# Attention, low-rank mix and MLP on one core: all 24 two-head steps ahead of the first layer, in a new order

## The chip, the cores and the metric

One core of a Trainium2 chip runs the whole program in one launch. The metric is device microseconds (us) of that core from the start to the end of an execution; 0.2% of it, about 1.8 us, is roughly what a measurement of this kernel can tell from no change.

## What is computed

The reference, cut to what matters (B = 4 batches, H = 12 heads, S = 448 positions, D = 64, model width 768, hidden width 3072, rank 32):

```python
scores = q @ k.T / sqrt(64)                    # per batch and head, causal mask
attn   = exp(scores - rowmax)
attn   = attn / (attn.sum(-1) + 1e-9)
x      = attn @ v                              # heads side by side: (B, S, 768)
h      = x.transpose(0, 2, 1) @ U @ V          # mix along the sequence, rank 32
u      = x + h.transpose(0, 2, 1)
out    = u + relu(u @ w_ch1) @ w_ch2           # 768 -> 3072 -> 768
```

## The kernel before

**Stages.** The program has three. First comes attention with the low-rank mix. Then the first layer (`mlp`) computes the MLP of batches 0 and 1, in 8 parts of 6 weight blocks: 192 small steps of 9 TensorE matmuls each, 1728 in all, each 128x128 by 128x448. Last comes the second layer (`strassen`), which does batches 2 and 3 with Strassen products. The weights arrive as 64-bit words that VectorE, ScalarE and GpSimd decode to 32-bit floats, block after block; a decoded block is written back to memory (`kept`) for the second layer.

**Attention.** The work is tiled in 24 pairs of heads (b, c), 6 per batch. A pair needs these operations, each a small function:

- `load_qk`, `load_v`: transfers, issued by SyncE (SP) in the order of the program.
- `scores` (L219): 8 score blocks of TensorE into six PSUM banks, tile `s`.
- `scores_max` (L234): VectorE scales, masks, takes the row maximum and writes `p` to SBUF, 8 times a pair (4 row tiles of 112 for each of 2 heads).
- `scores_exp` (L248): ScalarE, 8 times. `sums_inverse` (L255 adds 1e-9, L256 reciprocal): VectorE, twice. `normalise` (L261): GpSimd, 8 times.
- `transposes` (L272): 20 TensorE transposes in six groups (two heads, three parts), tile `t`; `transposed` copies each group from PSUM to `pt` in SBUF, three parts a head, the table `ENG` naming the engine (L164 ScalarE, L166 VectorE).
- `values` (L288): TensorE, tile `pv`; `values_out` (L164): ScalarE copies it to `x` (tiles `xa`, `xb`).
- `x_natural` (L320): four TensorE transposes of `x`, tile `xt`; `natural_high` (L324, ScalarE) and `natural_low` (L329, VectorE) split them into a high and a low part, `xn_h` and `xn_l`.
- For every second pair `low_rank` (L337, TensorE, tile `y`) and its split (L346 ScalarE, L350 VectorE).
- For each batch, when its six pairs are through, six times `mix` (L355, L356, TensorE, tile `hm`) and `mix_sum` (L360, VectorE); for batches 0 and 1 also `split_u` and `split_u_low` (L168, L172, GpSimd), the operands of the first layer.

**What sets the order.** Nothing is scheduled by the compiler: each engine runs its instructions in the order in which Python emits them. `attention()` makes the list `todo` from a table `plan`. In step n every operation works on pair n minus its lag: scores, maxima and exponentials lag 0, transposes lag 1, values and `x` transposes lag 2, low rank lag 3, mix later. In the old table one operation of `plan` is emitted for all its tiles at once. The list is cut at `START = 18`: steps 0 to 17 run ahead of the first layer, and the rest is emitted in pieces between the matmul groups of the first layer, spread over its first 132 small steps (`UFREE = 60` of 192 stay free). After it `u_rounds` prepares operands of the second layer, one round every `UGAP = 3` small steps. PSUM tiles come from a pool of 8 banks, shared by attention and first layer. The decoding of U and V (`low_rank_weights`) and of weight blocks 0 and 1 (`decode_w`) is put behind whole steps (`VU_AT`, `W_AT`).

Of the kernel before, what the change touches and what calls it, by code (L numbers as in the profile page):

```python
# [12 lines left out]
I32 = mybir.dt.int32  # L13
U32 = mybir.dt.uint32
AF = mybir.ActivationFunctionType
# [4 lines left out]
P = 128  # L20
# [20 lines left out]


ENG = {
    "h0": "A", "h1": "A", "h2": "V", "vc": "A",
    "uh": "P", "ul": "P",
}

MIX, MIXN = 4, 2
START = 18
VU_AT = (0, 2, 3, 4)
UFREE = 60
UGAP = 3
LOADS = (13, 11, 7)
PREPS = (7, 5, 3)

WE = "PVVP"
HE = {"d": "V", "o": "V", "13": "V", "24": "V"}  # L60
UE = {"d": "P", "o": "P", "13": "P", "24": "V"}
WL_AT = (1, 2)
W_AT = (7, 8, 9, 10, 11)


@with_exitstack
def attention_mix_mlp(ctx: ExitStack, tc: tile.TileContext, qk, v, w1, w2, vu, out):
# [26 lines left out]
    def apool(name, bufs, **kw):  # L94
        return att.enter_context(tc.tile_pool(name=name, bufs=bufs, side="right", **kw))

    const = apool("const", 1)
    p_qk = apool("p_qk", 3)
    p_v = apool("p_v", 2)
    p_pt = apool("p_pt", 2)  # L100
    p_p = apool("p_p", 4)
    p_sm = apool("p_sm", 6)
# [13 lines left out]
    def f(ap):  # L116
        return ap.bitcast(F32)
# [23 lines left out]
        nc.sync.dma_start(out=t[:, :n].rearrange("p a b -> p (a b)"), in_=src.bitcast(U32))  # L141
        return t

    def decode_bits(t, n):

        lo, hi = t[:, :n, 0], t[:, :n, 1]
        st["nwa"] = st.get("nwa", -1) + 1
        a = main.tile([P, WB], U32, tag=f"wa{st['nwa'] % 2}", name="wa")[:, :n]
        nc.scalar.activation(f(a), f(hi), AF.Abs)
        nc.vector.tensor_scalar(f(a), f(a), HI_MIN, HI_MAX, op0=ALU.max, op1=ALU.min)  # L150
        nc.vector.tensor_scalar(a, a, 3, 0x3FFFFFF8, op0=ALU.logical_shift_left, op1=ALU.bitwise_and)
        nc.vector.scalar_tensor_tensor(hi, hi, 0xC0000000, a, op0=ALU.bitwise_and, op1=ALU.bitwise_or)  # L152
        nc.scalar.activation(lo.bitcast(I32), lo, AF.Copy, scale=2.0**-29)
        return a

    def decode_sum(t, a, n):
# [17 lines left out]
    def split(src, hi, lo):  # L174
        nc.scalar.copy(hi, src)  # L175
        nc.vector.tensor_tensor(lo, src, f(hi), op=ALU.subtract)  # L176

    def low_rank_weights(step):
        if step == 0:
            st["vu"] = load_words(vu, VCOLS)  # L180
        elif step == 1:
            st["vua"] = decode_bits(st["vu"], VCOLS)
        elif step == 2:
            decode_sum(st.pop("vu"), st["vua"], VCOLS)
        else:
            a = f(st.pop("vua"))
            split(a[:, :S], vm_h, vm_l)
            u = a[:CP, S:].rearrange("p (s r) -> p s r", s=NT)
            for i in (0, 2):
                split(u, um_s[:, :, i, :], um_s[:, :, i + 1, :])  # L190

    def load_qk(b, c):

# [79 lines left out]
    def transposed(b, h, part):  # L275
        n = (4, 3, 3)[part] * CP
        t = st["pt", b, h, part] = p_pt.tile([CP, n], F32, tag=f"pt{part}", name="pt")
        copy(f"h{part}", t, st.pop(("t", b, h, part))[:, :n])

    def values(b, c):  # L280
        v = st.pop(("v", b, c))
# [102 lines left out]
    def load_w(n):  # L384
        if n < len(blocks):
            st["wr", n] = load_words(blocks[n], WB)

    def decode_w(n, step):
        if n >= len(blocks):
            return  # L390
        if step == 0:
            st["wa", n] = decode_bits(st["wr", n], WB)
        elif step == 1:
            decode_sum(st.pop(("wr", n)), st["wa", n], WB)
            nc.sync.dma_start(out=kept[n], in_=f(st["wa", n]))
        else:
            o = NC * 2 * S + n % 2 * 2 * WB
            wh, wl = wsp[:, o : o + WB], wsp[:, o + WB : o + 2 * WB]
            split(f(st.pop(("wa", n))), wh, wl)
            st["w", n] = wh, wl  # L400

    def decode_ahead(blk, quarter):
        if quarter == 0:
# [463 lines left out]

    def attention():


        def of_pair(f, lag):
            def steps(n):
                if 0 <= n - lag < len(pairs):
                    yield f, pairs[n - lag]

            return steps

        def of_tiles(f, half, lag, tiles):
            def steps(n):
                if 0 <= n - lag < len(pairs):  # L880
                    b, c = pairs[n - lag]
                    for i in tiles:
                        yield f, (b, 2 * c + half, i)

            return steps

        def of_head(f, half, lag):
            def steps(n):
                if 0 <= n - lag < len(pairs):
                    b, c = pairs[n - lag]  # L890
                    yield f, (b, 2 * c + half)

            return steps

        def of_two(f, lag):
            def steps(n):
                if 0 <= n - lag < len(pairs) and (n - lag) % 2:
                    b, c = pairs[n - lag]
                    yield f, (b, c // 2)

            return steps

        def mixes(f, part):
            def steps(n):
                for b in range(B):
                    for c in range(NC):
                        if n == b * NPAIR + NPAIR - 1 + MIX + c // MIXN and c % MIXN == part:
                            yield f, (b, c)

            return steps  # L910

        def only(f, *a):
            b, _ = a
            if b < 2:
                f(*a)

        def third(half):
            plan = []
            for i in range(3):
                plan.append(of_tiles(transposes, half, 1, (i,)))  # L920
                plan.append(of_tiles(transposed, half, 1, (i,)))
            return plan

        first, second = (0, 2, 3, 1), (1, 3, 2, 0)
        plan = [
            of_pair(load_qk, -2),
            of_pair(scores, 0),
            of_tiles(scores_max, 0, 0, first),
            of_tiles(scores_exp, 0, 0, first),
            of_pair(natural_low, 3),  # L930
            of_tiles(scores_max, 1, 0, second),
            of_tiles(scores_exp, 1, 0, second[:2]),
            of_pair(values, 2),
            of_pair(values_out, 2),
            of_head(sums_inverse, 0, 0),
            of_tiles(normalise, 0, 0, first),
            *third(0),
            of_tiles(scores_exp, 1, 0, second[2:]),
            of_pair(x_natural, 2),
            of_head(sums_inverse, 1, 0),  # L940
            of_tiles(normalise, 1, 0, second),
            *third(1),
            of_two(low_rank, 3),
            of_two(low_rank_high, 3),
            of_two(low_rank_low, 3),
            of_pair(natural_high, 2),
        ]
        for part in range(MIXN):
            plan += [mixes(mix, part), mixes(mix_sum, part)]
        plan.append(of_pair(load_v, 1))  # L950
        for part in range(MIXN):
            plan += [mixes(lambda *a: only(split_u, *a), part), mixes(lambda *a: only(split_u_low, *a), part)]

        def scores_and_max(b, c):
            scores(b, c)
            for half, i in SCORES:
                scores_max(b, 2 * c + half, i)

        def nothing(*_):
            pass  # L960

        among = {scores: scores_and_max, scores_max: nothing}
        todo = []
        for n in range(-2, len(pairs) + 8):
            for steps in plan:
                todo += [(n, f if n < START else among.get(f, f), a) for f, a in steps(n)]
        return todo

    with tc.manual_schedule():
        constants()  # L970
        early = [(n, low_rank_weights, (i,)) for i, n in enumerate(VU_AT)]
        early += [(n, load_w, (i,)) for i, n in enumerate(WL_AT)]
        for n, steps in zip(
            W_AT,
            (
                [(decode_w, (0, 0))],
                [(decode_w, (0, 1)), (load_w, (2,))],
                [(decode_w, (0, 2))],
                [(decode_w, (1, 0))],
                [(decode_w, (1, 1)), (load_w, (3,))],  # L980
            ),
        ):
            early += [(n, step, a) for step, a in steps]
        early.sort(key=lambda e: e[0])
        todo = attention()
        while todo[0][0] < START:
            n, step, a = todo.pop(0)
            step(*a)
            while early and early[0][0] <= n:
                _, step, a = early.pop(0)  # L990
                step(*a)


        steps = 4 * FS * (FC + NC // 2)
        free = steps - UFREE
        done = 0
        us = None
        for i, _ in enumerate(mlp()):
            while done < len(todo) and done * free < len(todo) * (i + 1):
                _, step, a = todo[done]  # L1000
                step(*a)
                done += 1
# [62 lines left out]
```

## Time and profile before

| what | value |
|---|---|
| time, median of 3 runs (lowest to highest) | 907.77 us (907.39 to 908.99) |
| the profiled execution: its own time | 908.52 us |
| the profiled execution: span of the profile | 906.7 us |
| granted TensorE clock, mean over the span | 0.982 of full speed |
| busy share: TensorE / VectorE / ScalarE / GpSimd | 96% / 75% / 52% / 35% |
| first matmul of the first layer | at 165.26 us |
| second layer begins | at 584.5 us |

Times inside the profile are us from the start of the span. The profile's span and the execution's own time differ by 1.8 us, which lies around the span. "Busy" of an engine is the time in which at least one of its instructions runs; TensorE's matmuls overlap one another, so the distance between the starts of two groups tells more than their durations. Engine names in rows: PE is TensorE (PEld its weight loads), DVE VectorE, ACT ScalarE, POOL GpSimd, SP SyncE.

### The profile page before, as it was taken

To read this page: it belongs to the slowest core of one execution; us is meant where nothing else is said; L and a number is where in the kernel's file an instruction comes from. 1 tells how busy PE (TensorE), PEld (TensorE's weight loads), DVE (VectorE), ACT (ScalarE), POOL (GpSimd) and SP (SyncE) were. 2 spreads that over 40 slices of the span, in tenths; PEclk is the share of its full clock that TensorE was granted. 3 is DMA by queue.
4 is the path that set the end of the run, shared out by engine and by line. 5 is a ranking of instruction groups with operands and counts; after the bars stand their busy time and mean duration, and the time that the engine had idled before them with its cause. 6 is when DMAs were issued, how large, how long until landed. Compare 5 with 4: busy or idle time off the path is not lost.

```text
span 906.7 us, 13562 instructions
## 1 busy us (share of the span) xinstructions
PE 868.4 (96%) x4728; PEld 759.0 (84%) x4728; DVE 681.3 (75%) x1368; ACT 474.9 (52%) x1002; POOL 318.8 (35%) x342
## 2 busy tenths in 40 slices
PE   6798889999999999999799999999999999999998
PEld 4676667888888888888699999998999898898887
DVE  5566767756666676756458788879988989988896
ACT  6888778644544545354234545365453635445530
POOL 4444756542223313131014334323423423423220
PEclk9899899999999999999999999999999999999999
DMA  7224143235444334344234445721211221212103
GB/s 247 63 82 124 43 133 93 74 123 169 153 139 161 132 119 153 130 143 146 83 105 157 157 167 199 240 58 56 85 53 35 86 67 42 74 47 71 35 1 122
DMA packets 47061, 98.99 MB, mean 109 GB/s; under 512 B 4240, under 2 KB 25744, under 8 KB 46992
## 3 DMA queue, kind: packets, MB, share of 16 engines
q1 hardware_dynamic: 46992, 98.12, 33.1%
q8 instruction: 37, 0.61, 0.3%
q14 instruction: 32, 0.26, 0.1%
HBM read 73.73 MB, written 24.38 MB: 108 GB/s over the span
## 4 chain that ended last, share of the span: by engine, by line
PE 39%; DVE 9%; ACT 2%; issue 1%; DMA 1%; SPq 0%; DVEq 0%; ACTq 0%
PE sa L656 13%; PE of L449 7%; PE hf L424 7%; PE se L656 7%; PE sb L656 3%; DVE h L470 2%; DVE tmp L470 1%; DVE sw L470 1%; DVE xb L470 1%; DVE wsp L470 1%; ACT h L478 1%; DVE r L470 1%; DMA v<-in_v_dram 1%; ACT wsp L593 0%; PE pv L288 0%
## 5 line engine op out<-in xcount | busy, mean ns | idle before, releaser
L449 PE MATMUL of<-g,wsp 128*128 128x448 f32 x864 | 184.5, 368 | 0.0
L470 POOL TENSOR_TENSOR wsp<-wld,wsp 128x512 fp32r<-128x512 f32 (+1 forms) x60 | 105.3, 1764 | 214.6 <-ACT wsp L593 131.4
L449 PEld LDWEIGHTS of<-g,wsp 128*128 128x128 f32 x864 | 159.9, 188 | 13.0 <-DVE g L433 0.2
L157 POOL TENSOR_TENSOR wa<-wld 128x768 int32<-128x768 int32 (+1 forms) x49 | 73.1, 1492 | 247.4 <-DVE wld L152 123.0
L261 POOL TENSOR_SCALAR p<-p,r 112x112 f32<-112x112 f32 (+1 forms) x192 | 99.7, 538 | 106.6 <-DVE r L256 55.2
L248 ACT ACTIVATE p<-p,m 112x112 f32<-112x112 f32 (+1 forms) x192 | 100.3, 525 | 28.8 <-DVE m L234 28.2
L656 PE MATMUL sa<-h,wsp 128*128 128x448 f32 x432 | 98.6, 367 | 1.9 <-DVE xb L470 1.9
L424 PE MATMUL hf<-u,wsp 128*128 128x448 f32 x432 | 96.4, 373 | 0.0
L424 PE MATMUL hf<-wsp 128*128 128x448 f32 x432 | 94.4, 368 | 0.0
L656 PE MATMUL sa<-uch,wsp 128*128 128x448 f32 x288 | 89.5, 371 | 3.4 <-ACT r L677 3.4
L656 PEld LDWEIGHTS sa<-h,wsp 128*128 128x128 f32 x432 | 80.6, 188 | 10.6 <-DVE xb L470 3.8
L424 PEld LDWEIGHTS hf<-u,wsp 128*128 128x128 f32 x432 | 80.9, 191 | 6.9
L452 DVE TENSOR_TENSOR xa<-of,xa 128x448 f32<-128x448 f32 x96 | 58.7, 620 | 36.8 <-PE of L449 36.4
L424 PEld LDWEIGHTS hf<-wsp 128*128 128x128 f32 x432 | 80.2, 188 | 7.0 <-issue 0.3
L234 DVE CUSTOM_DVE_ANT_0 p<-s,mask 112x112 f32<-112x112 f32 (+2 forms) x192 | 74.2, 444 | 14.1 <-PE s L219 12.3
L175 ACT CAST wsp<-wa 128x768 fp32r<-128x768 f32 x48 | 40.2, 837 | 83.8 <-POOL wa L157 75.6
L433 DVE SCALAR_TENSOR_TENSOR g<-hf,g 128x448 fp32r<-128x448 f32 x48 | 29.9, 623 | 62.5 <-ACT g L432 62.4
L432 ACT ACTIVATE g<-hf 128x448 fp32r<-128x448 f32 x48 | 26.2, 546 | 78.0 <-PE hf L424 77.9
L272 PE MATMUL t<-ident,p 112*112 112x112 f32 x480 | 63.2, 272 | 3.7 <-POOL p L261 2.1
L176 DVE TENSOR_TENSOR wsp<-wa,wsp 128x768 fp32r<-128x768 f32 x48 | 50.3, 1048 | 19.8 <-ACT wsp L175 19.2
L656 PEld LDWEIGHTS sa<-uch,wsp 128*128 128x128 f32 x288 | 54.0, 188 | 11.6 <-ACT r L677 6.6
L593 ACT CAST wsp<-sw 128x256 fp32r<-128x256 f32 (+3 forms) x60 | 33.9, 576 | 55.2 <-DVE sw L470 25.8
(93 smaller groups left out, 1633.4 us busy)
## 6 DMA issues: line engine op xcount, KB each, us to landing
wld<-in_w_dram SPq DMA_DIRECT2D x48, 768.0 KB, 4.6
kept<-wa SPq DMA_DIRECT2D x48, 384.0 KB, 2.6
qk<-in_qk_dram SPq DMA_DIRECT2D x24, 448.0 KB, 3.5
wld<-kept SPq DMA_DIRECT2D x24, 384.0 KB, 3.0
wld<-kept SPq DMA_DIRECT2D x72, 128.0 KB, 2.4
v<-in_v_dram SPq DMA_DIRECT2D x24, 224.0 KB, 4.8
out_dram<-xa SPq DMA_DIRECT2D x12, 224.0 KB, 2.3
out_dram<-xb SPq DMA_DIRECT2D x12, 224.0 KB, 1.9
```

The costliest lines, as they stand in the source:

```text
L157: nc.gpsimd.tensor_tensor(a.bitcast(I32), t[:, :n, 1].bitcast(I32), t[:, :n, 0].bitcast(I32), op=ALU.add)
L175: nc.scalar.copy(hi, src)
L176: nc.vector.tensor_tensor(lo, src, f(hi), op=ALU.subtract)
L234: nc.vector.tensor_tensor_reduce(out=st["p", b, h][:, POFF[i] : POFF[i] + n], in0=st.pop(("o", b, h, i)), in1=mask[:, S - n :], scale=-(D* ...
L248: nc.scalar.activation(pi, pi, AF.Exp, bias=m[:, i : i + 1], scale=-1.0, accum_out=l[:, i : i + 1])
L261: nc.gpsimd.tensor_scalar(pi, pi, r[:, i : i + 1], 1.0, op0=ALU.mult, op1=ALU.mult)
L272: nc.tensor.transpose(o[:, n : n + CP], src, ident[:CP, :CP])
L424: nc.tensor.matmul(o, a[:, cs], m, start=(kc + n == 0), stop=(kc + n == NC + 1))
L449: nc.tensor.matmul(o, a[:, cs], m, start=(fc + n == 0), stop=(fc + n == FC + 1))
L452: nc.vector.tensor_tensor(x, o, x, op=ALU.add)
L470: (nc.vector if e == "V" else nc.gpsimd).tensor_tensor(o, a, b, op=op)
L656: nc.tensor.matmul(st[bank, q], a, b, start=(n in FIRST and ms[0] == 0 and k == 0), stop=(n in LAST and end and k == len(steps) - 1), skip ...
```

## The change

The table `plan` is replaced by `PLAN`, a list of single operations: name, lag, and for `m`, `e`, `n` (maximum, exponential, normalise) the head and row tile, for `t` and `h` (transposes and their copies) the head and part, for `r` the head. All steps 0 to 23 are emitted ahead of the first layer; what still lags (the last pair's transposes and values, the last three `x` transposes, two low-rank products, nine mixes) is spread over the first 60 small steps of the first layer (`DRAIN`). `x` transposes now lag 3 instead of 2, and a mix is emitted once a step. The copies of transposes go to VectorE for the first head of a pair and to ScalarE for the second, where ScalarE had parts 0 and 1 and VectorE part 2 of both. The decoding of U, V and blocks 0 and 1 is cut into its nine operations (`decode_bit`, `weight_piece`), each with a step and a slot ("x") in `EARLY`. There is a fourth buffer for q and k and a third for v. `u_rounds` comes every 7 small steps.

```diff
 ENG = {
-    "h0": "A", "h1": "A", "h2": "V", "vc": "A",
+    "h00": "V", "h01": "V", "h02": "V", "h10": "A", "h11": "A", "h12": "A", "vc": "A",
     "uh": "P", "ul": "P",
 }
-MIX, MIXN = 4, 2
-START = 18
-VU_AT = (0, 2, 3, 4)
-UFREE = 60
-UGAP = 3
+PLAN = [
+    ("xp", 3), ("s", 0), ("x", 2), ("ua", 6), ("m", 0, 0, 0), ("m", 0, 0, 2), ("xh", 3),
...
+]
+EARLY = {
+    "vu": ((1, 2), (2, 0), (2, 0), (2, 0), (2, 3), (3, 2), (3, 2), (3, 3), (3, 3)),
...
+}
+LATER = ((12, 2, 2), (16, 3, 3))
+DRAIN = 60
+UGAP = 7
-WL_AT = (1, 2)
-W_AT = (7, 8, 9, 10, 11)
-    p_qk = apool("p_qk", 3)
-    p_v = apool("p_v", 2)
+    p_qk = apool("p_qk", 4)
+    p_v = apool("p_v", 3)
+    def weight_piece(n, piece):
+        if piece == 0:
+            load_w(n)
+        elif piece < 6:
+            st["wa", n] = decode_bit(st["wr", n], WB, piece - 1, st.get(("wa", n)))
+        elif piece == 6:
+            decode_w(n, 1)
+        else:
...
+            if piece == 7:
+                nc.scalar.copy(wh, f(st["wa", n]))
+            else:
+                nc.vector.tensor_tensor(wl, f(st.pop(("wa", n))), f(wh), op=ALU.subtract)
-    copy(f"h{part}", t, st.pop(("t", b, h, part))[:, :n])
+    copy(f"h{h % 2}{part}", t, st.pop(("t", b, h, part))[:, :n])
-        for n in range(-2, len(pairs) + 8):
-            for steps in plan:
-                todo += [(n, f if n < START else among.get(f, f), a) for f, a in steps(n)]
+        for n in range(-3, len(pairs) + 14):
+            for name, lag, *part in PLAN:
+                if name == "x":
+                    todo += [(n, step, a) for step, a in early.get((n, lag), ())]
+                    continue
...
-        while todo[0][0] < START:
-            n, step, a = todo.pop(0)
+        while todo[0][0] < len(pairs):
+            _, step, a = todo.pop(0)
             step(*a)
-            while early and early[0][0] <= n:
-                _, step, a = early.pop(0)
-                step(*a)
-        free = steps - UFREE
-            while done < len(todo) and done * free < len(todo) * (i + 1):
+            while done < len(todo) and done * DRAIN < len(todo) * (i + 1):
```

What it moves, at three places. First TensorE, a step in the middle of attention from its last three value products on (`pv` values, `t` transposes of `p`, `xt` transposes of `x`, `hm` mix, `s` scores). Before (a second mix follows, and then the next step's scores):

```order
L288 MATMUL pv<-pt,v 64x336
L288 MATMUL pv<-pt,v 64x224
L288 MATMUL pv<-pt,v 64x112
L272 MATMUL t<-ident,p 112x112 x10
L320 MATMUL xt<-ident,xa 112x128 x4
L272 MATMUL t<-ident,p 112x112 x10
L355 MATMUL hm<-vm_h,y 128x448
L356 MATMUL hm<-vm_l,y 128x448
```

And now:

```order
L313 MATMUL pv<-pt,v 64x336
L313 MATMUL pv<-pt,v 64x224
L313 MATMUL pv<-pt,v 64x112
L297 MATMUL t<-ident,p 112x112 x13
L380 MATMUL hm<-vm_h,y 128x448
L381 MATMUL hm<-vm_l,y 128x448
L297 MATMUL t<-ident,p 112x112 x7
L345 MATMUL xt<-ident,xb 112x128 x4
L244 MATMUL s<-qk 112x112
```

The transposes of `x` no longer stand between the two heads' transposes, behind the copy of the `pv` of the same step; they open the next step, and work on the pair before.

Second VectorE, from the last maximum of a step to the first of the next (`l` and `r` sums and reciprocals, `pt` copies of transposes, `y` low rank). Before:

```order
L234 ISA p,m<-s,mask 112x112
L234 ISA m 112x1
L255 TENSOR_SCALAR l<-l 112x4
L256 RECIPROCAL r<-l 112x4
L166 COPY pt<-t 112x336
L255 TENSOR_SCALAR l<-l 112x4
L256 RECIPROCAL r<-l 112x4
L166 COPY pt<-t 112x336
L350 TENSOR_TENSOR y<-y 64x256
```

And now:

```order
L280 TENSOR_SCALAR l<-l 112x4
L281 RECIPROCAL r<-l 112x4
L259 ISA p,m<-s,mask 112x336
L259 ISA m 112x1
L354 TENSOR_TENSOR xn_l<-xt,xn_h 112x4x128
L189 COPY pt<-t 112x336
L189 COPY pt<-t 112x448
L189 COPY pt<-t 112x336
L280 TENSOR_SCALAR l<-l 112x4
L281 RECIPROCAL r<-l 112x4
L375 TENSOR_TENSOR y<-y 64x256
```

The first reciprocal stands one maximum earlier, the second behind three copies; there is a third copy, of 448 columns.

Third TensorE at the start of the first layer (`hf` is its first product). Before:

```order
L424 MATMUL hf<-wsp 128x448 x9
L219 MATMUL s<-qk 112x112
L219 MATMUL s<-qk 112x224
L219 MATMUL s<-qk 112x336
L219 MATMUL s<-qk 112x448 x2
```

And now:

```order
L465 MATMUL hf<-wsp 128x448 x9
L345 MATMUL xt<-ident,xb 112x128 x4
L465 MATMUL hf<-wsp 128x448 x9
L465 MATMUL hf<-u,wsp 128x448 x9
L313 MATMUL pv<-pt,v 64x112
```

No scores stand between the groups of the first layer any more, only what lags.

## Rows read from the trace of the kernel before

**Rows 1.** Busy time of each engine in the three stages (windows).

```profile
core 0: us, PE busy (x) PEld busy (x) DVE busy (x) ACT busy (x) POOL busy (x), PEclk, DMA share, GB/s
0.00:165.26 165.26, 141.67 (x1028) 107.85 (x1029) 108.13 (x439) 130.04 (x405) 91.43 (x172) 0.93 0.35 111
165.26:584.30 419.04, 413.41 (x2189) 368.93 (x2188) 289.92 (x508) 197.53 (x351) 128.54 (x114) 0.99 0.43 146
584.30:906.70 322.40, 313.33 (x1514) 282.17 (x1512) 283.25 (x423) 147.37 (x247) 98.82 (x58) 1.00 0.20 61
```

**Rows 2.** PE in order of time (timeline: start, us, work, idle before): step 13, the layer's start.

```profile
124.77 0.36 PE L337 MATMUL y<-xn_h,um_s 112*128 112x256 f32 x1
...
125.89 2.15 PE L219 MATMUL s<-qk 64*112 64x112 f32 x16
127.96 2.11 PE L288 MATMUL pv<-pt,v 112*64 112x112 f32 x16
130.00 1.17 PE L272 MATMUL t<-ident,p 112*112 112x112 f32 x10
131.35 0.65 PE L320 MATMUL xt<-ident,xa 128*112 128x128 f32 x4 [0.18 <-ACT xa L164]
131.84 1.12 PE L272 MATMUL t<-ident,p 112*112 112x112 f32 x10
132.89 2.15 PE L219 MATMUL s<-qk 64*112 64x112 f32 x16
...
165.26 1.98 PE L424 MATMUL hf<-wsp 128*128 128x448 f32 x9
```

**Rows 3.** PE timeline of the start, from step 2 to step 4.

```profile
24.99 1.10 PE L320 MATMUL xt<-ident,xa 128*112 128x128 f32 x4 [2.30 <-ACT xa L164]
25.88 2.07 PE L272 MATMUL t<-ident,p 112*112 112x112 f32 x10
27.89 3.58 PE L219 MATMUL s<-qk 64*112 64x112 f32 x16
...
36.33 2.15 PE L219 MATMUL s<-qk 64*112 64x112 f32 x16
```

**Rows 4.** Who waited for whom, 0 to 165 us (total, times, longest).

```profile
DVE l L255 <- ACT p L248: 25.2, 18, 2.1
...
PE xt L320 <- ACT xa L164: 11.6, 11, 2.3
```

**Rows 5.** Groups by line and shape, 0 to 165 us (busy, mean ns).

```profile
L234 DVE CUSTOM_DVE_ANT_0 p<-s,mask 112x448 f32<-112x448 f32 x36 | 22.3, 620 | 1.2 <-PE s L219 1.2
...
L164 ACT COPY pt<-t 112x448 f32<-112x448 f32 x34 | 18.1, 532 | 0.9 <-PE t L272 0.9
...
L166 DVE COPY pt<-t 112x336 f32<-112x336 f32 x34 | 16.6, 490 | 8.4 <-PE t L272 8.4
```

**Rows 6.** PE timeline in the first layer: two dense groups, a stall, two mixes.

```profile
171.17 3.81 PE L424 MATMUL hf<-u,wsp 128*128 128x448 f32 x18
174.82 3.81 PE L424 MATMUL hf<-wsp 128*128 128x448 f32 x18
...
443.54 3.76 PE L288 MATMUL pv<-pt,v 112*64 112x112 f32 x16 [4.08 <-DMA v<-in_v_dram]
...
453.52 0.38 PE L337 MATMUL y<-xn_l,um_s 112*128 112x256 f32 x1 [1.12 <-DVE xn_l L329]
...
454.74 3.26 PE L424 MATMUL hf<-u,wsp 128*128 128x448 f32 x9
457.83 0.36 PE L355 MATMUL hm<-vm_h,y 128*128 128x448 f32 x1
...
458.24 0.36 PE L355 MATMUL hm<-vm_h,y 128*128 128x448 f32 x1
```

**Rows 7.** One slow sum on DVE, the GpSimd instruction beside it (timelines), and its line.

```profile
118.40 0.73 DVE L255 TENSOR_SCALAR l<-l 112x4 f32<-112x4 f32 x1
...
117.96 1.14 POOL L172 TENSOR_TENSOR wsp<-xa,wsp 128x448 fp32r<-128x448 f32 x1
...
L255 DVE TENSOR_SCALAR l<-l x36: 157/170/730, 10.4 to 164.7; 112x4 f32<-112x4 f32 x36
```

More of the change, by code (lines that the diff above doesn't have):

```diff
@@ L142, in load_words, with decode_bit @@
         return t
-    def decode_bits(t, n):
[L146 to L153, printed above, removed]
+    def decode_bit(t, n, piece, a=None):
+        lo, hi = t[:, :n, 0], t[:, :n, 1]
+        if piece == 0:
+            st["nwa"] = st.get("nwa", -1) + 1
+            a = main.tile([P, WB], U32, tag=f"wa{st['nwa'] % 2}", name="wa")[:, :n]
+            nc.scalar.activation(f(a), f(hi), AF.Abs)
+        elif piece == 1:
+            nc.vector.tensor_scalar(f(a), f(a), HI_MIN, HI_MAX, op0=ALU.max, op1=ALU.min)
+        elif piece == 2:
+            nc.vector.tensor_scalar(a, a, 3, 0x3FFFFFF8, op0=ALU.logical_shift_left, op1=ALU.bitwise_and)
+        elif piece == 3:
+            nc.vector.scalar_tensor_tensor(hi, hi, 0xC0000000, a, op0=ALU.bitwise_and, op1=ALU.bitwise_or)
+        else:
+            nc.scalar.activation(lo.bitcast(I32), lo, AF.Copy, scale=2.0**-29)
+        return a
+    def decode_bits(t, n):
+        a = None
+        for piece in range(5):
+            a = decode_bit(t, n, piece, a)
         return a
@@ L176, in split, with low_rank_weights @@
         nc.vector.tensor_tensor(lo, src, f(hi), op=ALU.subtract)
-    def low_rank_weights(step):
-        if step == 0:
+    def low_rank_weights(piece):
+        if piece == 0:
             st["vu"] = load_words(vu, VCOLS)
-        elif step == 1:
-            st["vua"] = decode_bits(st["vu"], VCOLS)
-        elif step == 2:
+        elif piece < 6:
+            st["vua"] = decode_bit(st["vu"], VCOLS, piece - 1, st.get("vua"))
+        elif piece == 6:
             decode_sum(st.pop("vu"), st["vua"], VCOLS)
         else:
-            a = f(st.pop("vua"))
-            split(a[:, :S], vm_h, vm_l)
+            a = f(st["vua"])
             u = a[:CP, S:].rearrange("p (s r) -> p s r", s=NT)
-            for i in (0, 2):
-                split(u, um_s[:, :, i, :], um_s[:, :, i + 1, :])
+            parts = [(a[:, :S], vm_h, vm_l)]
+            parts += [(u, um_s[:, :, i, :], um_s[:, :, i + 1, :]) for i in (0, 2)]
+            for src, hi, lo in parts:
+                if piece == 7:
+                    nc.scalar.copy(hi, src)
+                else:
+                    nc.vector.tensor_tensor(lo, src, f(hi), op=ALU.subtract)
     def load_qk(b, c):
@@ L400, in decode_w @@
             st["w", n] = wh, wl
+    def weight_piece(n, piece):
+        if piece == 0:
+            load_w(n)
+        elif piece < 6:
+            st["wa", n] = decode_bit(st["wr", n], WB, piece - 1, st.get(("wa", n)))
+        elif piece == 6:
+            decode_w(n, 1)
+        else:
+            o = NC * 2 * S + n % 2 * 2 * WB
+            wh, wl = wsp[:, o : o + WB], wsp[:, o + WB : o + 2 * WB]
+            st["w", n] = wh, wl
+            if piece == 7:
+                nc.scalar.copy(wh, f(st["wa", n]))
+            else:
+                nc.vector.tensor_tensor(wl, f(st.pop(("wa", n))), f(wh), op=ALU.subtract)
     def decode_ahead(blk, quarter):
@@ L868, in attention @@
     def attention():
[L871 to L962, printed above, removed]
@@ L963, in attention @@
-        todo = []
-        for n in range(-2, len(pairs) + 8):
-            for steps in plan:
-                todo += [(n, f if n < START else among.get(f, f), a) for f, a in steps(n)]
+        by_pair = {
+            "ld": load_qk, "s": scores, "lv": load_v, "v": values, "vc": values_out,
+            "xp": x_natural, "xh": natural_high, "xl": natural_low,
+        }
+        by_part = {
+            "m": scores_max, "e": scores_exp, "r": sums_inverse, "n": normalise,
+            "t": transposes, "h": transposed,
+        }
@@ new lines, in attention @@
+        by_two = {"lp": low_rank, "lh": low_rank_high, "ll": low_rank_low}
+        by_batch = {"ma": mix, "mb": mix_sum, "ua": split_u, "ub": split_u_low}
+        early = {}
+        for of, at in EARLY.items():
+            for piece, (n, slot) in enumerate(at):
+                step = (low_rank_weights, (piece,)) if of == "vu" else (weight_piece, (of, piece))
+                early.setdefault((n, slot), []).append(step)
+        for n, slot, block in LATER:
+            early.setdefault((n, slot), []).append((load_w, (block,)))
@@ new lines, in attention @@
+        todo = []
+        for n in range(-3, len(pairs) + 14):
[3 more added lines that the diff above has]
+                    continue
+                if name in by_batch:
+                    b, c = divmod(n - lag - NPAIR + 1, NC)
+                    if 0 <= b < B and not (b >= 2 and name in ("ua", "ub")):
+                        todo.append((n, by_batch[name], (b, c)))
+                    continue
+                if not 0 <= n - lag < len(pairs):
+                    continue
+                b, c = pairs[n - lag]
+                if name in by_pair:
+                    todo.append((n, by_pair[name], (b, c)))
+                elif name in by_part:
+                    todo.append((n, by_part[name], (b, 2 * c + part[0], *part[1:])))
+                elif c % 2:
+                    todo.append((n, by_two[name], (b, c // 2)))
@@ L970, in attention_mix_mlp @@
         constants()
[L971 to L984, printed above, removed]
         todo = attention()
-        while todo[0][0] < START:
-            n, step, a = todo.pop(0)
+        while todo[0][0] < len(pairs):
+            _, step, a = todo.pop(0)
             step(*a)
-            while early and early[0][0] <= n:
-                _, step, a = early.pop(0)
-                step(*a)
         steps = 4 * FS * (FC + NC // 2)
-        free = steps - UFREE
         done = 0
```

10 rows, old and new, of tables (EARLY, PLAN) are left out of this document.

## The prediction

> **What bounds the kernel now.** I read the stages first, then TensorE in order of time, then the waits, then the groups by line. In the stages [rows 1] TensorE is busy for 413 of 419 us in the first layer and 313 of 322 in the second: those two are bound by it. Attention is not: 142 of 165 us, at a granted clock of 0.93 of full speed, while ScalarE is busy for 130, VectorE for 108 and GpSimd for 91. So there, and only there, TensorE loses much time, and what it loses is found in its timeline.
>
> A dense step shows what a step needs [rows 2]. From start to start: scores 125.89 to 127.96, 2.07 us; values 2.04; ten transposes 1.17 (1.35 less 0.18 idle); transposes of `x` 0.49; ten transposes 1.05. Together 6.82. A low-rank product (124.77 to 125.89) adds 1.12, a mix 0.41 (457.83 to 458.24 [rows 6]). Steps 13 to 17 hold two low-rank products and six mixes: 5 x 6.82 + 2 x 1.12 + 6 x 0.41 = 38.8 us, and took 165.26 - 125.89 = 39.4. There the old order already runs at TensorE's speed, 0.1 us over it a step. Steps 4 to 17 hold seven low-rank products and twelve mixes, 14 x 6.82 + 7.8 + 4.9 = 108.2, and took 165.26 - 36.33 = 128.9 [rows 2, 3]: 20.7 us lost, 1.5 a step. Where it goes is in the waits [rows 4]: `xt` for the copy of `x` on ScalarE, 11 times, up to 2.3 us; and after such a wait the same work goes at the half clock: `xt` 1.10 for 0.65, transposes 2.07 for 1.12, scores 3.58 for 2.15 [rows 2, 3].
>
> **The sum, stage by stage.**
>
> *Attention, steps 0 to 3.* The first transfer, the first softmax and the filling of the pipeline stay as they are. Step 4 began at 36.33. In step 2 the wait of `xt` for `x` (2.30) falls away, since `x` is now transposed one step after its copy; with it the slow clock behind it, (1.10 - 0.65) + (2.07 - 1.12) + (3.58 - 2.15) = 2.8. So step 4 begins at 36.3 - 5.1 = 31.2. The decoding of U and V lies in steps 2 and 3 on ScalarE and VectorE as before; what it costs there is in the 36.33. Bounds: 29 (everything dense from step 2 on) to 36.3.
>
> *Attention, steps 4 to 23.* Twenty steps with all their parts, 20 x 6.82 = 136.4; low rank in ten of them, 11.2; a mix in each from 9 on, fifteen, 6.2. Sum 153.8. I add 0.12 a step for small waits, as in steps 13 to 17: 2.4. The layer then begins at 31.2 + 153.8 + 2.4 = 187.4, where it began at 165.26: +22.1.
>
> This holds only if no other engine needs more than the mean step of 7.7 us. Scaling the busy time of eighteen old steps to twenty-four [rows 1]: ScalarE 130.0 x 24/18 = 173 us, less 23 copies of 448 columns at 0.53 [rows 5], 161, 6.7 a step. VectorE 108.1 x 24/18 = 144, plus 23 such copies. It has no such row; bounds are its copy of 336, 0.49, and its maximum over 448, 0.62 [rows 5]. I take 0.60, since it is a copy of that length from PSUM: 158, 6.6 a step, with the decoding. GpSimd 122, 5.1 a step. So TensorE stays the longest by 1 us. What could still hold it is the order: the banks of a step's scores are freed by copies that stand in the second half of the step before, `pt` on VectorE before the second reciprocal, the last one on ScalarE just after the last transposes; TensorE needs 0.5 us for `xt` and one to two for the first scores ahead of that last bank. It is tight on VectorE, not late.
>
> Transfers: `v` and `qk` are issued two steps ahead, 15 us, and a further buffer each lets them start without waiting for the reader. Stores of decoded blocks stand in the same SP queue, each waiting for GpSimd, with the next `v` behind it; two steps of lead cover that, so I cost it at nothing. Without that cover it would cost what the stall in the first layer costs, below. The decoding pieces move whole instructions and add none.
>
> *First layer.* Dense, 18 matmuls take 174.82 - 171.17 = 3.65 us [rows 6], so 1728 take 350.4. Between them stood six scores (12.4), eight values (16.3), seven pairs of transposes (2.22 each, 15.5), eight transposes of `x` (3.9), five low-rank products (5.6), twelve mixes (4.9): 58.6. Together 409.0, and it took 419.0. Of the missing 10.0 the rows show 8.0: `pv` waited 4.08 for `v`, whose transfer stood late in the SP queue, then ran 3.76 for 2.11; `y` waited 1.12; nine matmuls took 454.74 to 457.83, 3.09, for 1.83 [rows 2, 6]. What still lags after the change: one pair's transposes 2.2, two values 4.1, three `x` 1.5, two low-rank 2.2, nine mixes 3.7: 13.7. Their inputs are ready some microseconds ahead, `v` included, so the stall goes; I leave 1 us for small waits. New length 350.4 + 13.7 + 1 = 365.1: -53.9. VectorE and ScalarE have less to do there than before. `u_rounds` now has 126 small steps instead of 54 and keeps its end.
>
> *Second layer.* None of its instructions moves: 322.4.
>
> Span 187.4 + 365.1 + 322.4 = 874.9, plus 1.8 around it, 876.7, against 908.5 of the profiled execution. That one lay 0.75 above the median of the runs, so **876** against 907.8, 3.5% less. The check: dense TensorE work is the same in both; what goes is 18 us lost in the old steps 4 to 17, 5 in the start, 9 in the first layer.
>
> **The rivals.**
>
> *The old losses stay.* Other waits take the place of that for `x`, and each step again loses 1.5 us with the half clock behind it: 31.2 + 153.8 + 20 x 1.5 = 215, in all 904. With half of it, 889. For it: three engines above 80% in lockstep, VectorE fuller than before. Against: steps 13 to 17 ran at TensorE's speed with ScalarE fuller than it will be.
>
> *VectorE's queue stops at the sums: slower than before.* Each step has two `l` sums that wait for ScalarE's exponentials, and behind the second in the queue stand mix sum, low-rank split and all maxima of the next step. Before, 18 of these waits took 25.2 us, 1.4 each, the longest 2.1 [rows 4]. If both in each step wait so, a step on VectorE is 6.6 + 2.8 = 9.4, twenty are 188, the layer begins at 219.2, and the time is 907.7, no change; at 2.1 each it is 10.8 a step and 936. It turns slower from 1.4 on. Against: one maximum now stands between the last exponential's release and the first sum, and three copies before the second.
>
> *VectorE and GpSimd hold each other up.* The sum over four columns took 0.73 us at 118.40, while a GpSimd instruction ran from 117.96 to 119.10; its median is 0.17 [rows 7]. In the denser step more of them would meet. If both sums of each step took 0.73, that is 1.1 us, VectorE at 7.7 would just equal TensorE, and with a few of its longer instructions held as well I price it at 8.2 a step: 31.2 + 164 = 195, in all 884. Against: the median over 36 of them. The Trainium skill, SBUF — State Buffer, section "SBUF: two separate sides", says that VectorE and GpSimd share one pair of ports by an exclusive lock, the loser waiting for the whole instruction of the other. The slow row agrees with that, the median says that they seldom meet; by the rule taken for every sum the time would be the rival's, by the rows the forecast's.
>
> *The first layer keeps its stall,* now on what lags (values behind a late copy, low rank behind a split): +9, 885.
>
> *The change doesn't do what it says:* a piece of block 0 or batch 1's operands, which GpSimd finishes only in step 23, come late and the layer waits at its start. The operands of one mix take GpSimd two instructions, the longer 1.14 us [rows 7], with the last normalisations around them; an estimate from that is 2 to 8 us: 878 to 884. For it: GpSimd runs about a step behind TensorE. Against: the first group uses batch 0, long ready.
>
> **How the numbers follow.** Forecast 0.60, old losses stay 0.16 (half of that chance below 893), VectorE's queue 0.05, VectorE and GpSimd 0.07, stall 0.07, late operands 0.05. Floor: start at 29, no small waits, 866.5; the range goes to 865. Upwards it takes in VectorE and GpSimd, stall, late operands and the milder half of the old losses: 893. Left out is about 0.13 above, and a little below. Of the outcomes, the forecast, VectorE and GpSimd, stall, late operands and old losses are faster by more than 0.2% (1.8 us); VectorE's queue is slower or level. Faster 0.94, same 0.02, slower 0.04.
>
> **What would show it.** Right: the first `hf` group near 187; steps from 4 on 6.8 to 8.4 us long; no wait of `xt` for the copy of `x`; clock near 1.0 from 30 us on; first layer 365 us long without a wait on `v`; second layer 322. Wrong: `hf` past 200 with PE idle before scores on a release by VectorE or ScalarE (old losses, or VectorE and GpSimd), maxima that start long after their scores (VectorE's queue), PE idle between groups of the first layer (stall), a second layer of another length.

## The result and the profile after

| | before | after |
|---|---|---|
| median of the runs (lowest to highest) | 908.38 us (907.39 to 909.28, 4 runs) | 865.92 us (865.57 to 866.27, 4 runs) |
| profiled execution, own time / span | 908.52 / 906.7 us | 866.12 / 864.3 us |
| attention, up to the first `hf` | 165.3 us | 177.6 us |
| first layer | 419.0 us | 363.6 us |
| second layer | 322.4 us | 323.1 us |

The ratio is 0.9533, 95% interval 0.9516 to 0.9549: 4.7% faster. The forecast was 876, its range 865 to 893. The three stages of the changed kernel, in busy time of each engine (as [rows 1]):

```profile
core 0: us, PE busy (x) PEld busy (x) DVE busy (x) ACT busy (x) POOL busy (x), PEclk, DMA share, GB/s
0.00:177.59 177.59, 172.09 (x1390) 134.20 (x1391) 150.47 (x606) 157.72 (x515) 115.00 (x222) 1.00 0.37 120
177.59:541.20 363.61, 363.61 (x1829) 335.36 (x1828) 254.42 (x366) 156.16 (x217) 94.51 (x63) 1.00 0.47 159
541.20:864.30 323.10, 313.93 (x1514) 282.42 (x1512) 282.57 (x423) 147.31 (x247) 99.88 (x58) 1.00 0.20 61
```

Attention now does a third more pairs in 12 us more. TensorE is busy for 172 of 178 us, at the full clock (1.00 for 0.93), and in the first layer it never stops. The other engines are fuller than before, ScalarE 89%, VectorE 85%. The sum had them at 161 and 158 us; they are at 158 and 150.

TensorE in order of time, where step 4 begins, then a step with neither low rank nor mix, and one with a mix (start, us, work):

```profile
28.73 0.60 PE L345 MATMUL xt<-ident,xa 128*112 128x128 f32 x4
...
51.09 0.60 PE L345 MATMUL xt<-ident,xa 128*112 128x128 f32 x4
51.62 2.15 PE L244 MATMUL s<-qk 64*112 64x112 f32 x16
53.70 2.11 PE L313 MATMUL pv<-pt,v 112*64 112x112 f32 x16
55.74 2.13 PE L297 MATMUL t<-ident,p 112*112 112x112 f32 x20
...
57.70 0.60 PE L345 MATMUL xt<-ident,xa 128*112 128x128 f32 x4
...
65.28 0.60 PE L345 MATMUL xt<-ident,xa 128*112 128x128 f32 x4
...
125.48 0.60 PE L345 MATMUL xt<-ident,xb 128*112 128x128 f32 x4
...
132.52 0.60 PE L345 MATMUL xt<-ident,xb 128*112 128x128 f32 x4
```

No row from 28.73 on shows an idle time before it, where [rows 2, 3] had 0.18 to 2.30 ahead of `xt`. A bare step takes 57.70 - 51.09 = 6.61 us, one with low rank 7.58, one with a mix 7.04. All waits of TensorE in attention:

```profile
PE s L244 <- DMA qk<-in_qk_dram: 4.4, 1, 4.4
PE t L297 <- POOL p L286: 1.0, 1, 1.0
PE s L244 <- DVE m L259: 0.2, 1, 0.2
```

All three lie in the start: the first transfer, the first normalisation, and a short wait for a maximum.

### The profile page after: what moved, and what is told of

Same layout as the page of the kernel before. It is cut to its first block, busy times and chain, and to the rows that moved or that the text cites. A ratio compares the mean times of both kernels' runs of the same rounds, so it can differ in the third digit from the quotient of the medians.

```text
span 864.3 us, 13588 instructions
## 1 busy us (share of the span) xinstructions
PE 849.6 (98%) x4728; PEld 752.0 (87%) x4728; DVE 687.5 (80%) x1392; ACT 461.2 (53%) x978; POOL 309.4 (36%) x342
## 4 chain that ended last, share of the span: by engine, by line
PE 87%; DVE 9%; ACT 2%; issue 2%; DMA 1%; DVEq 0%; ACTq 0%
PE hf L465 20%; PE of L490 20%; PE sa L697 15%; PE se L697 7%; PE s L244 6%; PE pv L313 6%; PE t L297 5%; PE sb L697 4%; DVE h L511 2%; DVE sw L511 2%; DVE tmp L511 1%; PE y L362 1%; PE xt L345 1%; DVE wsp L511 1%; DVE xb L511 1%
## 5 line engine op out<-in xcount | busy, mean ns | idle before, releaser
L490 PE MATMUL of<-g,wsp 128*128 128x448 f32 x864 | 177.7, 366 | 0.0
L490 PEld LDWEIGHTS of<-g,wsp 128*128 128x128 f32 x864 | 162.1, 188 | 12.6
L286 POOL TENSOR_SCALAR p<-p,r 112x112 f32<-112x112 f32 (+1 forms) x192 | 94.1, 507 | 61.6 <-DVE r L281 25.1
L273 ACT ACTIVATE p<-p,m 112x112 f32<-112x112 f32 x192 | 99.7, 525 | 13.6 <-DVE m L259 13.6
L465 PE MATMUL hf<-u,wsp 128*128 128x448 f32 x432 | 92.3, 366 | 0.0
L259 DVE CUSTOM_DVE_ANT_0 p<-s,mask 112x112 f32<-112x112 f32 (+1 forms) x192 | 74.6, 442 | 20.9 <-PE s L244 19.4
L634 ACT CAST wsp<-wld 128x512 fp32r<-128x512 f32 (+1 forms) x60 | 41.8, 703 | 38.1 <-PE sa L697 28.6
```

What stands on the lines that cost most here:

```text
L259: nc.vector.tensor_tensor_reduce(out=st["p", b, h][:, POFF[i] : POFF[i] + n], in0=st.pop(("o", b, h, i)), in1=mask[:, S - n :], scale=-(D* ...
L273: nc.scalar.activation(pi, pi, AF.Exp, bias=m[:, i : i + 1], scale=-1.0, accum_out=l[:, i : i + 1])
L286: nc.gpsimd.tensor_scalar(pi, pi, r[:, i : i + 1], 1.0, op0=ALU.mult, op1=ALU.mult)
L465: nc.tensor.matmul(o, a[:, cs], m, start=(kc + n == 0), stop=(kc + n == NC + 1))
L490: nc.tensor.matmul(o, a[:, cs], m, start=(fc + n == 0), stop=(fc + n == FC + 1))
L634: return lambda: nc.scalar.copy(st["ws", q, key][0], src())
```

## The experiments

The theory was that the waits of TensorE in a step, and the half clock behind them, are the loss, and that moving six steps ahead only moves dense work. The rivals stand in the expectations. Five kernels start from the old order, the other seven from the new. Runs of the kernel before beside them had medians of 906.4 to 907.0 us, against 908.4 in the result, so the whole gain is 40.5 to 42.5 us, 41 below. A difference of 1 or 2 us from the 865.9 of the change, which was measured apart from these kernels, says little.

### The cut alone

```diff
-START = 18
+START = 24
```

> The old order with all 24 steps ahead of the first layer (START 24), nothing else. Theory (the order of a step is what counts, the cut alone moves TensorE work from one dense place to another): six more steps with 0.1 to 1.5 us of loss each, the stall of 10 us in the first layer gone: 899 to 907 us, first layer from about 212 to 221. Rival (freeing the first layer of attention is the gain): 885 us or less.

Measured: 900.4 us, ratio 0.9924 (0.9906 to 0.9942). The stages, columns as above:

```profile
0.00:210.37 210.37, 185.27 (x1400) 142.02 (x1401) 145.51 (x586) 172.32 (x540) 117.65 (x224) 0.95 0.32 100
210.37:576.14 365.77, 365.77 (x1818) 333.43 (x1816) 255.91 (x361) 155.77 (x216) 95.53 (x62) 1.00 0.47 159
```

As the theory has it. The first layer falls to 365.8, 53.3 us less, since the values that stalled on `v` are no longer in it; attention, at 210.4, takes 45.1 of that back. Its waits are the old ones:

```profile
PE xt L320 <- ACT xa L164: 11.4, 10, 2.3
...
PE pv L288 <- DMA v<-in_v_dram: 3.2, 1, 3.2
```

### The transposes of x a step later, in the old order

```diff
-            of_pair(x_natural, 2),
+            of_pair(x_natural, 3),
```

and likewise one more for `natural_high`, `natural_low`, the three of low rank, `MIX` and `START`.

> The old order with the transposes of x, their split, the low rank and the mix one step later, and the cut one step later so that batch 1 is ready for the first layer. Theory (the wait of xt for the copy of x, and the half clock behind it, are the loss of the attention stage): 15 to 25 us less, 884 to 893 us, no xt wait of over 0.5 us left. Rival (other waits take its place): over 900 us.

Measured: 892.0 us, ratio 0.985 (0.9753 to 0.9947). Nineteen steps end at 162.0 us, where eighteen had ended at 165.3. TensorE's waits in that stretch:

```profile
PE pv L288 <- DVE l L255: 4.2, 1, 4.2
PE s L219 <- DMA qk<-in_qk_dram: 4.0, 1, 4.0
PE t L272 <- DVE m L234: 3.0, 4, 1.5
PE t L272 <- POOL p L261: 2.4, 3, 1.3
PE pv L288 <- DMA v<-in_v_dram: 1.9, 1, 1.9
```

No wait of `xt` is among them, and the time lies within the theory's range, at its upper end. In part other waits took its place: values waited 4.2 us once (the releaser named is inferred) and 1.9 for `v`.

### v a step earlier, in the old order

```diff
-    p_v = apool("p_v", 2)
+    p_v = apool("p_v", 3)
...
             of_pair(load_qk, -2),
+            of_pair(load_v, 0),
...
-        plan.append(of_pair(load_v, 1))
```

> The old order with a third buffer for v and its transfer issued a step earlier, right behind that of q and k. Theory: the wait of 4.1 us for v in the first layer goes with its slow clock, some 9 us, and the one of 3.0 us at 115 us with about 1 us of slow clock: 895 us. Rival (the transfer is late because of the stores ahead of it in the queue, whatever its buffer): 904 us or more.

Measured: 893.2 and 898.2 us, ratio 0.9891 (0.9776 to 1.0007), so not clear of no change by the interval. The profile shows what went: TensorE waits for `v` in neither place any more, the first layer takes 411.8 us (419.0), attention 156.5 (165.3).

```profile
0.00:156.53 156.53, 136.07 (x1028) 104.54 (x1029) 108.92 (x439) 129.52 (x405) 91.43 (x172) 0.96 0.39 120
156.53:568.29 411.76, 410.20 (x2189) 367.46 (x2188) 288.94 (x508) 196.78 (x351) 127.53 (x114) 1.00 0.43 147
```

The 8.8 us in attention are twice what was expected there; the stage's clock is 0.96 for 0.93, and how often it falls differs between executions of the old order (last section).

### The three together

> The old order with the three edits together: 24 steps ahead, x one step later, v early. Theory (these are the whole of the gain, operations placed one at a time add little): first layer from 178 to 190 us, 868 to 878 us. Rival (the fine order, or the new engines of the copies, is needed for a dense step): 885 us or more.

Measured: 879.8 us, ratio 0.9716 (0.9623 to 0.9809), between theory and rival. First layer 363.7 as after the change, attention 192.6 for 177.6:

```profile
0.00:192.59 192.59, 179.53 (x1393) 136.18 (x1394) 140.95 (x582) 169.02 (x539) 117.73 (x224) 1.00 0.35 111
```

So some 27 of the 41 us come without the fine order and without the new engines of the copies. ScalarE is busy for 169 us here and for 158 after the change, which the next kernel follows up.

### The new order with the old engines of the copies

```diff
-    "h00": "V", "h01": "V", "h02": "V", "h10": "A", "h11": "A", "h12": "A", "vc": "A",
+    "h00": "A", "h01": "A", "h02": "V", "h10": "A", "h11": "A", "h12": "V", "vc": "A",
```

> The new order with the old engines for the copies of transposes (ScalarE parts 0 and 1 of both heads, VectorE part 2). Theory (TensorE sets the step, ScalarE and VectorE both have room): at most 2 us more, 866 to 868 us. Rival (ScalarE becomes the bound, or the first head's copies now stand behind exponentials and hold banks): 0.5 us a step, 876 us or more.

Measured: 875.3 us, ratio 0.9655 (0.9627 to 0.9683): 9.3 us more, close to the rival's 876. VectorE's largest wait, then ScalarE and VectorE in one step:

```profile
DVE l L280 <- ACT p L273: 37.3, 24, 2.3
```

```profile
115.28 0.88 ACT L187 COPY pt<-t 112x448 f32<-112x448 f32 x2 [0.43 <-PE t L297]
116.04 0.55 ACT L187 COPY xb<-pv 128x448 f32<-128x448 f32 x1
116.47 0.69 ACT L273 ACTIVATE p<-p,m 112x448 f32<-112x448 f32 x1
...
117.13 0.58 ACT L273 ACTIVATE p<-p,m 112x336 f32<-112x336 f32 x1
...
117.83 0.17 DVE L280 TENSOR_SCALAR l<-l 112x4 f32<-112x4 f32 x1 [1.78 <-ACT p L273]
```

The first head's copies stand on ScalarE ahead of the last two exponentials; ScalarE waits 0.43 us for their transposes, the exponentials come later, and the second sum on VectorE holds its queue for 1.8 us. After the change that wait is 2.0 us in all. It is of the kind that the prediction's rival on the slower side names, once a step instead of twice, but it is not shown to cost TensorE anything. The chain of work that ended last has no VectorE in it from 100 to 180 us, only TensorE and ScalarE (shares of that stretch):

```profile
by line: PE s L244 29.2%; PE pv L313 25.5%; PE t L297 21.5%; PE xt L345 6.7%; PE y L362 6.6%; ACT pt L187 4.4%; ACT xb L187 2.2%; PE hm L380 1.7%; PE hm L381 1.5%; issue 0.8%; ACTq L187 0.1%
```

And TensorE's weight loads for the scores wait for ScalarE's copies of `pt`, here and after the change:

```profile
PEld s L244 <- ACT pt L187: 6.7, 21, 0.9
...
PEld s L244 <- ACT pt L187: 0.7, 2, 0.4
```

So it is the other reason that the expectation gives: ScalarE copies late, and the banks of the next scores come free late. The transposes of `x` wait for their copy too, 2.0 us in four steps.

### The lag of the x transposes, in the new order

```diff
-    ("xp", 3), ("s", 0), ("x", 2), ...
+    ("s", 0), ("x", 2), ...
-    ("t", 1, 1, 2), ("ma", 4), ("h", 1, 0, 1), ("vc", 2), ...
+    ("ma", 4), ("h", 1, 0, 1), ("vc", 2), ("xp", 2), ("t", 1, 1, 2), ...
```

> The new order with the transposes of x two steps behind instead of three, emitted after values_out of the same step and between the two heads' transposes, as in the old order; their split stays where it is. Theory (what matters is that the copy of x is done when TensorE arrives; here it stands behind six exponentials, 0.5 us before or after the three transposes end): a wait of 0.2 to 0.8 us in each step, 870 to 882 us, with the clock still full. Rival (the lag alone is the gain): 885 us or more. Rival (the lag is worth nothing in the new order): 867 us or less.

Measured: 866.2 us, the time of the change itself; the second rival holds. TensorE waits for the copy of `x` twice, 0.7 us together:

```profile
PE xt L345 <- ACT xa L187: 0.7, 2, 0.5
```

The same lag on top of the old engines of the copies:

> The new order with both the old engines of the copies (875.3 alone) and the transposes of x at lag 2 between the heads' transposes (866.2 alone). Theory (with more copies on ScalarE the copy of x ends late, and only then does the lag count): more than the sum, xt waits of 0.5 us or more in most steps, the half clock behind them, 882 us or more. Rival (the two are independent): 875 to 877 us.

Measured: 894.9 us, ratio 0.9868 (0.9816 to 0.992), 28.9 above the change, where the two edits alone cost 9.3 and 0.2. Waits of TensorE, then attention:

```profile
PE xt L345 <- ACT xa L187: 15.6, 12, 1.5
PE xt L345 <- ACT xb L187: 9.3, 9, 1.0
```

```profile
0.00:207.78 207.78, 175.66 (x1395) 133.68 (x1395) 137.96 (x582) 172.80 (x539) 118.62 (x222) 0.99 0.31 103
```

So the wait for `x` needs both: a copy that ends late because ScalarE carries four copies of transposes, and a transpose in the same step. Either edit of the change alone takes nearly all of it away (2.0 us are left with the old engines, 0.7 with the old lag). The half clock that I expected behind these waits did not come (0.99), though they sum to 25 us.

### Room on VectorE

```diff
     t = st["pt", b, h, part] = p_pt.tile([CP, n], F32, tag=f"pt{part}", name="pt")
+    if h % 2 == 0 and part == 0:
+        for _ in range(3):
+            nc.vector.tensor_copy(t, st["t", b, h, part][:, :n])
```

> The new order with the 448 copy of the first head made four times instead of once, 1.6 us more for VectorE in each of 23 steps. Theory (VectorE waits about 0.9 us a step for scores, 1.5 with low rank; beyond that it sets the step): 0.2 to 0.6 us a step, 870 to 880 us. Rival (VectorE already sets the step): 1.6 us a step, 900 us. Rival (it has far more room): within 1 us of 866.

Measured: 890.0 us, ratio 0.9818 (0.979 to 0.9847), midway between what I expected, 880 at most, and the rival's 900.

```profile
116.81 1.94 DVE L305 COPY pt<-t 112x448 f32<-112x448 f32 x3
118.78 1.04 DVE L189 COPY pt<-t 112x448 f32<-112x448 f32 x2
```

```profile
PE s L244 <- DVE pt L189: 14.5, 13, 1.6
```

The three copies cost 118.78 - 116.81 = 1.97 us, not 1.6, and the span grew by 23.7 us, 1.03 in each of 23 steps. So VectorE had about 0.9 us of room a step, close to the idle time that it shows after the change ahead of the first maximum:

```profile
134.21 0.28 DVE L259 CUSTOM_DVE_ANT_0 p<-s,mask 112x112 f32<-112x112 f32 x1 [0.92 <-PE s L244]
```

### The decoding in clumps

```diff
-    "vu": ((1, 2), (2, 0), (2, 0), (2, 0), (2, 3), (3, 2), (3, 2), (3, 3), (3, 3)),
+    "vu": ((1, 2), (2, 1), (2, 1), (2, 1), (2, 1), (2, 1), (3, 1), (4, 2), (4, 2)),
```

and blocks 0 and 1 in the same way, at steps 7 to 9, and 10 and 11.

> The new order with the decoding of U and V and of blocks 0 and 1 in clumps again: five operations in one slot of steps 2, 7 and 10, the split of U and V in step 4, of block 0 in step 9. Theory (a clump holds VectorE 2.2 us and ScalarE 1.8 us, against about 1 us of room in a step, three times): 2 to 6 us more, 868 to 872 us. Rival (placing them one at a time is worth nothing): within 1 us of 866.

Measured: 870.0 us, ratio 0.9597 (0.9569 to 0.9624): 4.0 us more, as expected; the first layer begins at 181.3 for 177.6. Three steps account for it: from scores to scores, steps 4, 8 and 11 take 1.5, 1.2 and 1.1 us longer than after the change, each one or two steps behind a clump.

### What lags, spread out; fewer buffers

```diff
-DRAIN = 60
-UGAP = 7
+DRAIN = 132
+UGAP = 3
```

> The new order with what lags spread over the first 132 small steps of the first layer instead of 60, and a round of u_rounds every 3 instead of 7. Theory (this work lies beside TensorE's wherever it stands): within 1 us of 866. Rival (early draining matters, rounds close together hold TensorE): 3 us or more above.

Measured: 869.7 us, ratio 0.9591 (0.9539 to 0.9643), 3.8 us more, as the rival has it. Attention is as after the change, the first layer 367.3 us for 363.6, and 2.6 us of the cost are one wait at its end:

```profile
544.38 0.71 PE L697 MATMUL sa<-uch,wsp 128*128 128x448 f32 x1 [2.58 <-DVE xa L493]
```

VectorE does the same work at nearly the same times there as after the change, its last add to `xa` at 543.6 (543.4). What differs is the bank: the emission order decides which of the eight PSUM banks a tile gets, and in the built program the layer's last `of` tile lies in bank 0 here, which the second layer's first product `sa` takes; after the change it lies in bank 1, which `sb` takes 2.6 us later, at a wait of 0.64. So most of the cost is a coincidence of banks, and not the spreading as such; the rival's number holds, its reason doesn't. The rest, about 1 us, was not traced.

```diff
-    p_qk = apool("p_qk", 4)
-    p_v = apool("p_v", 3)
+    p_qk = apool("p_qk", 3)
+    p_v = apool("p_v", 2)
...
-    ("m", 0, 0, 3), ("m", 0, 1, 0), ("m", 0, 0, 1), ("m", 0, 1, 1), ("lv", 0), ("e", 0, 0, 0),
+    ("m", 0, 0, 3), ("m", 0, 1, 0), ("m", 0, 0, 1), ("m", 0, 1, 1), ("e", 0, 0, 0),
...
-    ("e", 0, 0, 2), ("e", 0, 0, 3), ("e", 0, 0, 1), ("m", 0, 1, 3), ("r", 0, 0), ("v", 2),
+    ("e", 0, 0, 2), ("e", 0, 0, 3), ("e", 0, 0, 1), ("m", 0, 1, 3), ("r", 0, 0), ("v", 2), ("lv", 0),
```

> The new order with three buffers for q and k and two for v, as before; the transfer of v is issued after the values of the same step, since its buffer is free only then. Theory (more than a step of lead is enough, it is the place in the SP queue that counts): within 1.5 us of 866. Rival (the buffers hide late transfers): 5 us or more above.

Measured: 871.3 us, ratio 0.9609 (0.9558 to 0.966), 5.4 more; the rival holds, by another road than it says. Nearly all of it is one event in step 7, which takes 4.5 us longer (the SP queue, ScalarE, TensorE):

```profile
48.69 0.42 SPq L153 DMA_DIRECT2D wld<-in_w_dram  x1
```

```profile
56.16 0.91 ACT L162 ACTIVATE wa<-wld 128x768 f32<-128x768 f32 x1 [4.54 <-DMA wld<-in_w_dram]
```

```profile
60.56 0.97 PE L297 MATMUL t<-ident,p 112*112 112x112 f32 x4 [3.51 <-DVE m L259]
```

With `v` issued once its buffer is free, the queue stands, and the load of block 1 behind it goes out at 48.69 instead of 42.51; ScalarE reaches the decoding in step 7 and stands 4.5 us. No transfer of `v` or of q and k was late.

### The new engines of the copies, in the old order

```diff
-    "h0": "A", "h1": "A", "h2": "V", "vc": "A",
+    "h00": "V", "h01": "V", "h02": "V", "h10": "A", "h11": "A", "h12": "A", "vc": "A",
```

on top of the three together.

> The old order with 24 steps ahead, x later, v early (879.8), and the new engines of the copies in addition. Theory (the engines of the copies are worth the same 9 us here, the rest up to 865.9 is the decoding placed one operation at a time): 869 to 872 us. Rival (without the fine order the copies on VectorE hold its queue): 878 us or more.

Measured: 876.7 us, ratio 0.9669 (0.9612 to 0.9725), between theory and rival. Attention falls by 7.0 us (185.6 for 192.6) of the 9 expected; the first layer takes 366.4, with the same wait of 2.6 us at its end, and the last `of` in bank 0 again.

```profile
0.00:185.64 185.64, 175.02 (x1393) 135.17 (x1393) 156.15 (x606) 160.81 (x517) 118.52 (x226) 1.00 0.36 115
```

What then parts it from the change in attention is 185.6 - 177.6 = 8.0. If the decoding costs here what it cost in the new order, 3.7, then 4.3 is left for the order inside a step and the fourth buffer of q and k, which were not tried by themselves.

## Why the prediction was right, and where it was off

**The mechanism held.** Three stages, TensorE the bound of all of them after the change, the loss in waits of the old steps and in the first layer's stall. Measured against the forecast, in span: step 4 begins at 28.7 (31.2), the layer at 177.6 (187.4), it takes 363.6 (365.1), the second layer 323.1 (322.4). The sum of the misses is -2.5 - 7.3 - 1.5 + 0.7 = -10.6: 864.3 for 874.9.

**The term that was mis-sized is that of steps 4 to 23:** 148.9 us for 156.2. I took 6.82 for a bare step; it is 6.61. The two rows of ten transposes [rows 2] were added as 1.17 and 1.05; twenty in one go take 57.70 - 55.74 = 1.96. The first row's end is that of its last transpose, with nothing started behind it, and not the place where the next could have begun. That is 0.21 a step, 4.2 us. A low-rank product costs 7.58 - 6.61 = 0.97 in the stream, not 1.12, 1.5 us over ten. The 0.12 a step for small waits was 2.4 us and should have been about 0.5, which is what the 148.9 have beyond 20 steps of 6.61, ten low-rank products and 15 mixes of 0.43 (0.41 forecast, -0.3). Together 4.2 + 1.5 + 1.9 - 0.3 = 7.3.

**The start** gained more than its wait and slow clock, 7.6 us for 5.1, and went just below the lower bound of 29. The filling of the pipeline did not stay as it was: the scores of step 2 begin at 14.81 for 15.94.

**The range held by luck.** Its floor was added wrongly: from the prediction's own terms it is 29 + 153.8 + 350.4 + 13.7 + 322.4 = 869.3 in span, plus 1.8 around it and less 0.75 to the median, so 870.4 and not 866.5. The measured 865.9 lies 4.5 us under that, and within the range only since the range went down to 865.

**The cause of the x wait was told too simply.** The prediction let it fall because of the lag, and put the half clock behind each such wait, which the last section shows to be too simple. The runs show that in the new order the lag is worth nothing that can be told (0.2 us); with fewer copies on ScalarE the copy of `x` is ready in the same step. In the old order the lag does it. Only with both undone does the wait come back, 25 us of it.

**The rivals.** The old losses did not stay, since both their conditions were removed. VectorE's queue did stop at the sums when the copies were put back on ScalarE, for 37 us of waiting; but the 9.3 us that this kernel lost lie on a chain of TensorE and ScalarE, so this rival's price was not seen. VectorE and GpSimd hardly held each other up: the sum's median is 0.169 us (0.170 before), its longest 0.864, and 48 of them took 9.6 us, 1.5 over what the median gives. The stall went with the cut, as the old order shows by itself (365.8). The operands of batch 1 were not late. "It is tight on VectorE, not late" came out as some 0.9 us of room a step.

**What the change is made of.** Undone one at a time, in us above 865.9: engines of the copies 9.3, buffers with `v` behind its values 5.4, decoding 4.0, drain and rounds 3.8 (2.6 of it by the bank of one tile), lag of `x` 0.2, copies and lag together 28.9. These don't add up to 41, and none of them is the gain by itself. From the other side, the cut, the lag of `x` and the early `v` bring 27 of it in the old order.

## What to carry to other kernels

Sum the bound engine's work from start to start in a stretch where it never stops; a row whose end is followed by a wait holds the tail of its last instruction. A wait with two conditions falls to either edit, so undo each alone and both together before naming a cause. In queues in order, ask of each instruction that may wait what stands behind it: here a late buffer held a weight load, and two copies ahead of two exponentials held a sum on VectorE. Whether such a hold costs anything is read from the chain that ended last and from what the bound engine waits for.

## What was not expected of the hardware

What a wait does to TensorE's clock differs from one wait to the next. In the kernel with the cut alone, `xt` waited 1.72 us at 89.31 and 2.17 at 101.53, and `pv` waited 3.16 at 118.03:

```profile
89.31 1.02 PE L320 MATMUL xt<-ident,xa 128*112 128x128 f32 x4 [1.72 <-ACT xa L164]
...
101.53 0.65 PE L320 MATMUL xt<-ident,xa 128*112 128x128 f32 x4 [2.17 <-ACT xa L164]
...
118.03 2.11 PE L288 MATMUL pv<-pt,v 112*64 112x112 f32 x16 [3.16 <-DMA v<-in_v_dram]
```

The granted clock of the 3 us behind the first was 0.52 of full speed, nearly all at the lower of the two levels (1.2 of 2.4 GHz); that of the 8 us behind each of the other two was 1.00. In the kernel before it was the other way round: behind the wait of 1.72 us at 89.21 the clock stayed at 1.00, and behind the one of 2.17 at 99.59 it was 0.50 for 6 us. Nor does it always fall at once: behind the wait of 2.16 us at 71.07 the four transposes still took 0.65 us, and from 71.70 to 73.30 the clock was 0.53.

In the new order with the old engines of the copies and the old lag, 21 waits of up to 1.5 us left the granted clock of the stage at 0.99. Nine runs of the kernel before beside the first experiments lay between 901.4 and 909.9 us, at mean clocks of 0.980 to 0.990, the four runs of the changed kernel between 865.6 and 866.3, all at 1.00. That the wider spread comes from waits that sometimes lower the clock is likely from these rows; it was not tried.
